# Where the block transposes of e stand in a unit: behind the first two fifths of its MLP work instead of in front of it

## The chip, the core and the metric

The kernel runs on one core of one Trainium2 chip. The metric is the device time of one execution in microseconds (us). Engines are named as in the profile: PE is TensorE (PEld its weight loads), DVE is VectorE, ACT is ScalarE, POOL is GpSimd, SP is SyncE, which in this kernel only issues DMAs. Each engine works off its own instructions in order, and waits on semaphores where an instruction needs the work of another engine.

## The reference

Thresholded attention feeds an MLP mixer. All data are float32; B = 8, H = 8 heads, S = 576, D = 64.

```python
scores = scale * np.matmul(q, k.transpose(0, 1, 3, 2))
thresh = np.max(scores, axis=-1, keepdims=True) - tau
scores = np.where(scores >= thresh, scores, -1000000000.0)
attn = softmax(scores)
attn_out = np.matmul(attn, v)                     # (B, H, S, D)
x = attn_out.transpose(0, 2, 1, 3).reshape(B, S, H * D)
xt = x.transpose(0, 2, 1)
h = np.maximum(xt @ w_tok1, 0.0) @ w_tok2
u = x + h.transpose(0, 2, 1)
out = u + np.maximum(u @ w_ch1, 0.0) @ w_ch2
```

## The kernel before, in words

**Units.** The attention is cut into 144 units, 18 for each batch: 128 queries of two heads, or, in every ninth half-batch unit (the "s" unit), the last 64 queries of four heads. The main loop at the end of the kernel takes a unit u at a time and emits, in this order: `scores(u)` (PE matmuls L301 into PSUM, the row maximum mx on DVE L306, the bias on POOL L307); `norm(u - 1)` (two small DVE operations, L330 and L331, then POOL scales e, L334); in batches 1 to 7 the transposes of unit w = u - 2; MLP work, `fill(0.4)`; `weigh(u)` (ACT L316 and L323, with three times `fill(0.2)` in between); loads of later heads; and `values` (PE L408 and L413, then ACT L418), which multiplies the transposed weights by v for a group of units that was transposed two units ago.

**The transposes.** Batch 0 transposes e on PE (`turn`). From batch 1 on `turn_blocks` does it: one DVE instruction of 128 x 1152 transposes the 32 x 32 blocks of e into T (L368). When the last unit of a group is done (a group is two units, or one s unit), 16 DMAs on SP's queue move the blocks to their places in eT (L378); call these 16 a train. 126 units go through `turn_blocks`, in 70 trains.

**The MLP work.** When a batch's attention is complete, `push` puts its MLP steps in a list, `todo`. A token step `tok2` is two PE matmuls (L446) and one DVE addition that takes the result out of PSUM (L450); `tok1` ends in an ACT operation (L440). A channel step `ch1` is four groups of matmuls (L468) that ACT takes out (L469); a `ch2` tile is four steps of matmuls (L480, L484) that DVE copies out (L489) and SP stores (L490). Where a batch's token steps meet channel steps left over from the batch before, they are interleaved. `fill(share)` takes steps until a share of the unit's quota of PE time is used, so two fifths of a unit's MLP work come in the first call, and three times a fifth inside `weigh`. During batch 1 the DVE also unpacks weights (`weight`, L201, L205, L209).

**PSUM of the MLP.** All MLP steps take their PSUM tile from one pool, `ps_mm`, of two buffers (banks 6 and 7). Which of the two a tile gets is decided when the program is built. Usually the two alternate; in some places a tile gets the buffer of the tile just before it, and its first matmul then waits until that one has been taken out.

These are the lines of the main loop that the change touches, with the two callees of interest:

```python
        if back:
            key, place, many = group_of(w)
            if in_blocks(key[0]):
                turn_blocks(w)
...
        if b_now:
            fill(0.4)
        weight(2 if b_now else 1)
        if on:
            weigh(u)
```

Of the kernel before, what the change touches and what calls it, by code (L numbers as in the profile page):

```python
# [21 lines left out]
def kernel(  # L22
# [144 lines left out]
    def load_piece(i):  # L167
        if i >= len(pieces):
            return
        dst, src = pieces[i]  # L170
        rows = dst.shape[0]
        n = 1
        for d in dst.shape[1:]:
            n *= d
        raw = raw_at[i % NRAW][0:rows, 0 : n * (2 if wide(i) else 1)].bitcast(src.dtype)
        nc.sync.dma_start(out=like(raw, dst), in_=src)
        if wide(i):
            words = raw.bitcast(U32).rearrange("p (n w) -> p n w", w=2)
            h2 = work.tile([P, WMAX], F32, tag="o", name=f"h2_{i}")[0:rows, 0:n]
            raws[i] = like(words[:, :, 0], dst), like(words[:, :, 1], dst), like(h2, dst)  # L180
        else:
            raws[i] = like(raw, dst)
# [4 lines left out]
    def on_scalar(i, part):  # L187
        if wide(i):
            lo, hi, h2 = raws[i]
            if part == 0:  # L190
                nc.scalar.activation(out=lo.bitcast(I32), in_=lo, func=AF.Copy, scale=2.0**-29)
            else:
                nc.scalar.activation(out=h2, in_=hi.bitcast(F32), func=AF.Square)

    def on_vector(i, part):
        if wide(i):
            dst = pieces[i][0]
            lo, hi, h2 = raws[i]
            bits = dst.bitcast(U32)
            if part == 0:  # L200
                nc.vector.tensor_scalar(  # L201
                    out=bits, in0=hi, scalar1=3, scalar2=0x3FFFFFFF, op0=ALU.logical_shift_left, op1=ALU.bitwise_and
                )
            elif part == 1:
                nc.vector.scalar_tensor_tensor(  # L205
                    out=bits, in0=hi, scalar=0xC0000000, in1=bits, op0=ALU.bitwise_and, op1=ALU.bitwise_or
                )
            else:
                nc.vector.scalar_tensor_tensor(out=dst, in0=h2, scalar=2.0**-30, in1=dst, op0=ALU.is_ge, op1=ALU.mult)  # L209

    def on_gpsimd(i):
        if i >= 0:
            dst = pieces[i][0]
            if wide(i):
                nc.gpsimd.tensor_tensor(out=dst.bitcast(I32), in0=dst.bitcast(I32), in1=raws.pop(i)[0].bitcast(I32), op=ALU.add)
            else:
                nc.gpsimd.tensor_copy(out=dst, in_=raws.pop(i))
# [5 lines left out]
    def weight(n):  # L223

        nonlocal steps_done
        for k in range(steps_done, min(steps_done + n, 3 * len(pieces) + 1)):
            i, part = divmod(k, 3)
            if part == 0:
                on_gpsimd(i - 1)
                if i:  # L230
                    load_piece(i - 1 + NRAW)
            else:
                on_scalar(i + 1, part - 1)
            on_vector(i, part)
            steps_done = k + 1
# [39 lines left out]
    def in_blocks(b):  # L275
        return b > 0
# [10 lines left out]
    def scores(u):  # L287
        b, p0, t = units[u]
        sc = [
            (ps_3rd if b == 0 and (2 * u + h) % 3 == 2 else ps_sc).tile([P, 2, MAIN], F32, tag="sc", name=f"sc{h}_{u}") for h in range(2)  # L290
        ]
        if t == SHARED:
            parts = [(b * NP + p0 + i, slice(MAIN, S), slice(64 * i, 64 * i + 64)) for i in range(2)]
        else:
            i, c = divmod(t - (t > SHARED), NI)
            parts = [(b * NP + p0 + i, slice(P * c, P * c + P), slice(0, P))]
        order = [(f, part, h) for f in range(2) for part in parts for h in range(2)]
        for f, (n, cols, rows), h in order if b else sorted(order, key=lambda o: o[2]):
            r = slice(D * h, D * h + D)
            qT, kT = heads[n]  # L300
            nc.tensor.matmul(sc[h][rows, f, 0:HS], lhsT=qT[r, cols], rhs=kT[r, HS * f : HS * f + HS], start=True, stop=True)  # L301
        mx = small.tile([P, 2], F32, tag="mx", name=f"mx_{u}")
        bias = small.tile([P, 2], F32, tag="bias", name=f"bias_{u}")
        for h in range(2):
            c = slice(h, h + 1)
            nc.vector.tensor_reduce(out=mx[:, c], in_=sc[h][:, :, 0:HS], axis=AX.XY, op=ALU.max)  # L306
            nc.gpsimd.tensor_scalar(out=bias[:, c], in0=mx[:, c], scalar1=toff, scalar2=-SCALE, op0=ALU.add, op1=ALU.mult)  # L307
        st[u] = sc, bias
# [28 lines left out]
    def group_of(u):  # L337

        b, p0, t = units[u]
        if t == SHARED:  # L340
            return (b, p0, "s"), 0, 1
        i, c = divmod(t - (t > SHARED), NI)
        return (b, p0 + i, c // 2), c % 2, 2
# [17 lines left out]
    def turn_blocks(u):  # L361

        key, place, n = group_of(u)
        e = st.pop(u)
        if place == 0:
            Ts[key] = work.tile([P, NK * 2 * P], F32, tag="T", name=f"T_{u}")
        T = Ts[key][:, 0 : NK * n * P]
        nc.vector.transpose(  # L368
            out=T.rearrange("p (a c n x) -> p c a n x", a=4, c=NK, n=n)[:, :, :, place, :],
            in_=e.rearrange("p (c a x) -> p c a x", c=NK, a=4),  # L370
        )
        if place == n - 1:
            del Ts[key]
            eTs[key] = work.tile([P, NK * 2 * P], F32, tag="eT", name=f"eT_{u}")
            w = NK * n * 32
            for a in range(4):
                for i in range(4):
                    nc.sync.dma_start(  # L378
                        out=eTs[key][32 * a : 32 * a + 32, w * i : w * i + w], in_=T[32 * i : 32 * i + 32, w * a : w * a + w]
                    )  # L380

    def split_middle(n):

        lv, vl = vals[n], vlast[n % VL]
        for h in range(2):
            r = slice(D * h, D * h + D)
            nc.gpsimd.tensor_copy(out=vl[r, r], in_=lv[r, NI, :])
        vals[n] = lv, vl
# [116 lines left out]
    def fill(share):  # L505
        nonlocal credit
        credit += share * quota
        while todo and credit > 0:
            cost, step = todo.popleft()
            credit -= cost  # L510
            step()
        if not todo:
            credit = 0.0
# [20 lines left out]
    for u in range(len(units) + LAG + 4):  # L534
        on = u < len(units)
        if u == UB:
            late.close()
            ps_mm = ctx.enter_context(tc.tile_pool(name="ps_mm", bufs=2, space=bass.MemoryType.PSUM))
        if on:
            b_now, p0, t = units[u]  # L540
            n = b_now * NP + p0
        w = u - LAG
        back = 0 <= w < len(units)
        if on:
            scores(u)
        if 0 < u <= len(units):
            norm(u - 1)
        if b_now:
            weight(2)
        if back:  # L550
            key, place, many = group_of(w)
            if in_blocks(key[0]):
                turn_blocks(w)
            else:
                for i in range(3):
                    turn(w, i)
            if place == many - 1:
                b, p, c = key
                if c == 0 and p % 2 == 0:
                    split_middle(b * NP + p)  # L560
                if c == "s":
                    split_middle(b * NP + p + 1)
                when = u + (2 if in_blocks(b) else 1)
                due += [(when, b, p + i, c) for i in range(2 if c == "s" else 1)]
        if b_now:
            fill(0.4)
        weight(2 if b_now else 1)
        if on:
            weigh(u)
        elif b_now:  # L570
            fill(0.6)
        weight(2 if b_now else 1)
        if on:
            m = n + 2 + t // 4
            if t < 8 and m < len(pairs):
                load_qk(m, (nc.scalar if b_now else nc.sync,) * 2, t % 4)
                if t % 4 == 3:
                    load_v(m)
            if t == 2:
                prep(n + 1)  # L580
            if t == 7 and n + 2 < len(pairs):
                prep(n + 2)
        while due and due[0][0] <= u:
            _, b, p, c = due.popleft()
            values(b, p, c)
            if p == NP - 1 and c == 1:
                push(b)
# [31 lines left out]
```

## Time and profile before

| what | value |
|---|---|
| median of 3 runs | 1394.02 us (1393.48 to 1395.14) |
| the profiled execution, its own time | 1392.27 us |
| span of its profile | 1390.5 us |
| granted TensorE clock, mean | 0.991 |
| DVE busy | 586.8 us, 42% of the span |
| ACT busy | 590.0 us, 42% |
| POOL busy | 357.8 us, 26% |
| transposes T<-e, L368 | x126, 1369 ns each |
| additions xT<-xT,t, L450 | x64, 441 ns each |
| copies o<-c, L489 | x36, 679 ns each |
| DMA issues eT<-T, L378 | x1120 on SP, about 2.0 us from issue to landing |

The span runs from the first to the last instruction; the 1.8 us between it and the time of the same execution lie around it. A row of the timeline reads: start in us, length in us, engine, line, operation, what is written and read, number of instructions merged in the row, and in brackets the idle time of the engine before it and what ended that. A row of the waits reads: who waited for whom, then us in total, times, and the longest in us.

### The profile page before, as it was taken

How to read it: one execution, taken by the hardware profiler on the slowest of the kernel's cores; microseconds unless marked ns; L12 is line 12 of the kernel's file. 1: busy time of each engine (PE TensorE's matmuls, PEld its weight loads, DVE VectorE, ACT ScalarE, POOL GpSimd, SP SyncE). 2: the span in 40 equal slices, each digit the busy share in tenths (PEclk: the TensorE clock that was granted, in tenths of full speed). 3: DMA queues.
4: the chain of work that ended last, by engine and by line, in shares of the span. 5: the costliest groups of instructions: out<-in, count | busy, mean ns of one | idle time of the engine just before them, and what ended most of it. 6: DMA issues, size and time to landing. Idle time of an engine off the chain costs nothing.

```text
span 1390.5 us, 19515 instructions
## 1 busy us (share of the span) xinstructions
PE 1325.5 (95%) x6866; PEld 831.8 (60%) x6866; DVE 586.8 (42%) x1009; ACT 590.0 (42%) x1328; POOL 357.8 (26%) x683
## 2 busy tenths in 40 slices
PE   6776899999999999999999999999999999999998
PEld 3443475646565566665766567465657566575675
DVE  6788784444444444434244344433343453101000
ACT  5776564444454444443434435353434444120110
POOL 4566563232222222212122222221221222000000
PEclk9998899999999999999999999999999999999999
DMA  6444654444444434433433444443433433300000
GB/s 132 97 115 125 185 140 122 109 120 93 107 118 107 105 86 97 109 84 79 110 85 92 104 96 102 98 105 79 99 91 89 103 76 85 84 8 16 8 8 23
DMA packets 257376, 128.34 MB, mean 92 GB/s; under 512 B 208064, under 2 KB 221376, under 8 KB 257280
## 3 DMA queue, kind: packets, MB, share of 16 engines
q1 hardware_dynamic: 131632, 111.46, 30.5%
q10 hardware_dynamic: 125648, 15.64, 7.1%
q8 instruction: 55, 0.90, 0.3%
q14 instruction: 41, 0.34, 0.1%
HBM read 43.25 MB, written 9.44 MB: 38 GB/s over the span
## 4 chain that ended last, share of the span: by engine, by line
PE 86%; DVE 6%; DMA 2%; ACT 2%; SPq 2%; POOL 1%; issue 1%; DVEq 0%; ACTq 0%
PE c L484 27%; PE c L468 26%; PE sc L301 11%; PE pv L413 7%; PE t L439 5%; PE t L446 3%; PE pv L408 2%; DVE mx L306 2%; PE tx L430 1%; SPq L378 1%; PE c L480 1%; PE pv_s L413 1%; DVE T L368 1%; DMA scratch<-in_moe_w_ch_dram 1%; ACT e L316 1%
## 5 line engine op out<-in xcount | busy, mean ns | idle before, releaser
L306 DVE TENSOR_REDUCE mx<-sc 128x1 f32<-128x576 f32 x288 | 204.7, 751 | 523.1 <-PE sc L301 521.1
L468 PE MATMUL c<-xT,wc 128*128 128x256 f32 (+1 forms) x1920 | 398.6, 361 | 0.5 <-ACT g L469 0.4
L484 PE MATMUL c<-wc,g 128*128 128x512 f32 x864 | 389.1, 596 | 0.0
L468 PEld LDWEIGHTS c<-xT,wc 128*128 128x128 f32 x1920 | 334.3, 190 | 69.7 <-issue 27.6
L307 POOL TENSOR_SCALAR bias<-mx,toff 128x1 f32<-128x1 f32 x288 | 79.6, 277 | 814.9 <-DVE mx L306 757.9
L316 ACT ACTIVATE e<-sc,bias 128x576 f32<-128x576 f32 x288 | 199.2, 739 | 155.5 <-POOL bias L307 155.1
L484 PEld LDWEIGHTS c<-wc,g 128*128 128x128 f32 x864 | 157.9, 190 | 175.3 <-issue 173.2
L469 ACT ACTIVATE g<-c 128x256 f32<-128x256 f32 (+1 forms) x240 | 86.7, 361 | 335.5 <-PE c L468 330.6
L334 POOL TENSOR_SCALAR e<-e,rr 128x576 f32<-128x576 f32 x288 | 218.8, 772 | 16.0 <-DVE rr L331 3.8
L323 ACT ACTIVATE e<-e,ntau 128x576 f32<-128x576 f32 x288 | 220.6, 771 | 0.0
L301 PE MATMUL sc<-kT,qT 64*128 64x288 f32 (+1 forms) x1280 | 190.1, 435 | 14.2 <-DVE kT L283 7.2
L368 DVE STREAM_TRANSPOSE T<-e 128x1152 f32<-128x1152 f32 x126 | 172.5, 1369 | 16.3 <-DMA eT<-T 9.6
L301 PEld LDWEIGHTS sc<-kT,qT 64*128 64x128 f32 (+1 forms) x1280 | 103.7, 179 | 90.0 <-issue 47.6
L413 PE MATMUL pv<-eT,lv 128*64 128x256 f32 x1024 | 123.5, 384 | 0.0
L413 PEld LDWEIGHTS pv<-eT,lv 128*64 128x64 f32 x1024 | 75.1, 139 | 37.5 <-issue 0.8
L489 DVE COPY o<-c 128x512 f32<-128x512 f32 x36 | 24.5, 679 | 160.8 <-PE c L484 160.8
L446 PE MATMUL t<-w,a 128*128 128x288 f32 x256 | 79.0, 438 | 13.6 <-DVE xT L450 10.4
L418 ACT COPY xT<-pv 128x256 f32<-128x256 f32 x64 | 23.8, 372 | 160.0 <-PE pv L413 147.2
L439 PE MATMUL t<-x_sb,w 128*128 128x512 f32 x160 | 73.2, 605 | 0.7 <-ACT g L469 0.7
L446 PEld LDWEIGHTS t<-w,a 128*128 128x128 f32 x256 | 46.8, 198 | 41.4 <-DVE xT L450 18.4
L450 DVE TENSOR_TENSOR xT<-xT,t 128x288 f32<-128x288 f32 x64 | 28.0, 441 | 81.9 <-PE t L446 81.9
L323 ACT ACTIVATION_READ_ACCUMULATOR e<-e,ntau 128x1 f32 x288 | 56.5, 196 | 0.0
(48 smaller groups left out, 603.2 us busy)
## 6 DMA issues: line engine op xcount, KB each, us to landing
eT<-T SPq DMA_DIRECT2D x896, 72.0 KB, 2.1
scratch<-in_moe_w_ch_dram SPq DMA_DIRECT2D x24, 512.0 KB, 4.0
lv<-in_v_dram SPq DMA_DIRECT2D x32, 288.0 KB, 3.3
out_dram<-o SPq DMA_DIRECT2D x36, 256.0 KB, 2.2
eT<-T SPq DMA_DIRECT2D x224, 36.0 KB, 1.9
lk<-in_k_dram ACTq DMA_DIRECT2D x108, 72.0 KB, 2.8
lq<-in_q_dram ACTq DMA_DIRECT2D x104, 72.0 KB, 2.1
lq<-in_q_dram SPq DMA_DIRECT2D x24, 72.0 KB, 3.4
```

The source lines that it names most:

```text
L301: nc.tensor.matmul(sc[h][rows, f, 0:HS], lhsT=qT[r, cols], rhs=kT[r, HS * f : HS * f + HS], start=True, stop=True)
L306: nc.vector.tensor_reduce(out=mx[:, c], in_=sc[h][:, :, 0:HS], axis=AX.XY, op=ALU.max)
L316: nc.scalar.activation(out=eh, in_=sc[h][:, :, 0:HS], func=AF.Prelu, bias=bias[:, h : h + 1], scale=SCALE, alpha=STEEP)
L323: nc.scalar.activation(out=eh, in_=eh, func=AF.Exp, bias=ntau, accum_out=rs[:, h : h + 1])
L334: nc.gpsimd.tensor_scalar(out=eh, in0=eh, scalar1=rr[:, h : h + 1], scalar2=1.0, op0=ALU.mult, op1=ALU.mult)
L368: nc.vector.transpose(out=T.rearrange("p (a c n x) -> p c a n x", a=4, c=NK, n=n)[:, :, :, place, :], in_=e.rearrange("p (c a x) -> p c a ...
L413: nc.tensor.matmul(to[r], lhsT=lv[:, j, :], rhs=eT[:, j], start=False, stop=(c == NI - 1), skip_group_check=True)
L439: nc.tensor.matmul(ps, lhsT=w1[:, t, P * m : P * m + P], rhs=x_sb[:, t, :], start=(t == 0), stop=(t == NT - 1))
L446: nc.tensor.matmul(ps, lhsT=s["a"][:, m, P * c : P * c + P], rhs=w2[:, m, HS * f : HS * f + HS], start=(m == 0), stop=(m == NTK - 1))
L468: nc.tensor.matmul(ps, lhsT=wc1[:, j, c, :], rhs=uT[:, c, GR * i : GR * i + n], start=(c == 0), stop=(c == NCC - 1))
L469: nc.scalar.activation(out=s["g"][:, j, 0:n], in_=ps, func=AF.Relu)
L484: nc.tensor.matmul(flat, lhsT=s["g"][:, j, P * t : P * t + P], rhs=wc2[:, j, :], start=False, stop=(j == NJ - 1), skip_group_check=True)
```

## The change

`turn_blocks(w)` is emitted behind `fill(0.4)` instead of in front of it. Batch 0's `turn` and the list of due `values` stay where they were; no instruction is added or taken away.

```diff
         if back:
             key, place, many = group_of(w)
-            if in_blocks(key[0]):
-                turn_blocks(w)
-            else:
+            if not in_blocks(key[0]):
                 for i in range(3):
                     turn(w, i)
             if place == many - 1:
...
         if b_now:
             fill(0.4)
+        if back and in_blocks(key[0]):
+            turn_blocks(w)
         weight(2 if b_now else 1)
         if on:
             weigh(u)
```

## The prediction, made before the changed kernel had been run

> **What bounds the kernel now.** I read the page's busy times first, then its slices.
>
> ```profile
> PE 1325.5 (95%) x6866; PEld 831.8 (60%) x6866; DVE 586.8 (42%) x1009; ACT 590.0 (42%) x1328; POOL 357.8 (26%) x683
> PE   6776899999999999999999999999999999999998
> PEclk9998899999999999999999999999999999999999
> ```
>
> PE is full from the sixth slice on (a slice is 34.8 us), and DVE, on which the moved instruction runs, is busy 42%. So a DVE instruction costs or gains time only where PE waits for what stands behind it. The waits of PE alone, from 140 to 1200 us, which covers the stretch with block transposes, show all there is to win:
>
> ```profile
> PE t L446 <- DVE xT L450: 10.4, 8, 2.6
> PE t L446 <- ACT g L469: 3.1, 6, 0.8
> PE sc L301 <- ACT e L316: 1.9, 1, 1.9
> PE c L480 <- ACT g L469: 0.7, 2, 0.4
> PE t L439 <- ACT g L469: 0.7, 2, 0.4
> PE c L468 <- ACT g L469: 0.4, 1, 0.4
> ```
>
> The first row is 10.4 us in eight waits for the token step's addition. The four ACT g rows, 4.9 us, look foreign to a change on DVE; I come back to them. The timeline at one wait of the first kind:
>
> ```profile
> 315.83 2.21 PE L446 MATMUL t<-w,a 128*128 128x288 f32 x8
> 317.46 0.17 DVE L331 RECIPROCAL rr<-rr 128x2 f32<-128x2 f32 x1
> 317.55 1.36 DVE L368 STREAM_TRANSPOSE T<-e 128x1152 f32<-128x1152 f32 x1
> 318.83 0.78 DVE L450 TENSOR_TENSOR xT<-xT,t 128x288 f32<-128x288 f32 x2
> 319.30 3.18 PE L446 MATMUL t<-w,a 128*128 128x288 f32 x12 [1.26 <-DVE xT L450]
> ```
>
> Two token steps fill both PSUM buffers by 318.04; the additions that would free them stand behind the transpose, which nothing needs soon. PE restarts 0.47 us after the addition's start. A wait also costs the overlap of two matmuls: L446 lasts 0.41 us but starts every 0.24 us, so a closed gap of 1.26 returns up to 1.42.
>
> **What moves.** In the order of the built programs PE, ACT and POOL have the same instructions in the same order. On DVE only 31 of the 126 transposes pass anything, because in the other units the first two fifths hold no DVE work: 19 pass one or two token additions, ten pass a copy o<-c, two pass one of each. Nothing passes a later unit's mx. On SP 8 of the 70 trains pass an output transfer. Dropped work: none; added work: none; so the sum consists of waits alone.
>
> **Where the addition is freed.** In each case the addition takes the transpose's start, and PE restarts 0.47 to 0.48 after that or when its previous matmuls end, whichever is later.
> - At 317.63: restart 318.03, returned 1.27; then the transpose lies 318.3 to 319.7 and holds the next addition, and the third step after loses about 0.1. Net 1.15.
> - At 326.69: addition at 326.60 instead of 328.23; 1.6.
> - At 489.3: addition at 488.25 (it doesn't share the transpose's 0.24 wait); all 0.79 of the gap and the overlap, 0.95.
> - At 620.8 and 944.7: 0.50 gap each, wholly, 0.67; two smaller delays of 0.16 in each of these batches (a matmul starting late without a listed gap) go too: 2.0 together.
> - At 477.0: the addition frees its step (1.04), but here the built program gives the next channel step the same buffer, so it waits for an addition of 0.45 and two hand-overs, estimated at 0.70. Net 0.35.
>
> **The ACT rows.** Here the position of the transpose decides the buffer:
>
> ```profile
> 803.42 1.05 PE L468 MATMUL c<-xT,wc 128*128 128x128 f32 x8
> 804.07 1.36 DVE L368 STREAM_TRANSPOSE T<-e 128x1152 f32<-128x1152 f32 x1
> 804.52 0.28 ACT L469 ACTIVATE g<-c 128x128 f32<-128x128 f32 x1 [2.95 <-PE c L468]
> 804.85 1.24 PE L446 MATMUL t<-w,a 128*128 128x288 f32 x4 [0.37 <-ACT g L469]
> 805.35 0.42 DVE L450 TENSOR_TENSOR xT<-xT,t 128x288 f32<-128x288 f32 x1
> ```
>
> The step at 804.85 has the buffer of the channel step just finished, and must wait until ACT has taken that out. In the changed program nine tiles that had their predecessor's buffer get the other one (one before, four in each of batches 4 and 6), and one tile (the one at 477) newly gets its predecessor's. The step at 804.85 then waits for the addition before it, moved to 804.07: restart 804.55, 0.30 returned. The same at 814.7 (0.29, and 0.24 at the next step) and 822.7 (0.30). At 780.4 the tile waits for a copy o<-c that also leaves the transpose's shadow: 0.45. That is 1.58 per batch, twice 3.2. The tile at 498 gets 0.5. The wait of 0.83 at 799 stays: there ACT is late by a bias, in both programs.
>
> **Batch 1's start, and the clock.** Gaps of 2.58 at 150.24 and 2.33 at 163.83 lie in the stretch where DVE unpacks weights. The first only moves: its transpose passes one addition of two, and the other stays at 154.5 behind L209 and L201, so the second next step starts at 155.0 as before: 0. At the second both additions pass; the first channel step then starts at about 168.5 instead of 169.8. DVE is busy 9.79 of 10 us at 175 to 185, and mx at 172.87 had waited only 1.04 for PE, so I carry 1.0 on. The windows there:
>
> ```profile
> 152.82:160.00 7.18, 7.18 (x26) 4.06 (x28) 4.34 (x7) 5.13 (x10) 2.30 (x2) 0.56 0.75 199
> 166.17:169.40 3.23, 3.23 (x7) 2.37 (x8) 2.19 (x4) 0.00 (x0) 3.06 (x4) 0.51 0.82 253
> ```
>
> The third number from the right is the granted clock: 0.56 and 0.51 after these gaps, some (1 - 0.56) x 7.18 = 3.2 and 1.6 us of PE time. The Trainium skill ("TensorE: Matmul & The Clock Gate", the section "Why this matters for your kernels") asks for no idle gaps over about 3 us; by it gaps of 2.6 and 2.3 cost no clock and shrinking them returns none. By the rows they do cost it, and up to 3 us more could return in the first stretch (the second's loss is inside the 1.0). Because the first stretch's idle time is only split, 1.3 and 2.4 us, I take 0 and keep 3 for the range. Below zero: if the halved window falls later, up to 1.0 is lost.
>
> **What comes later.** The moved transpose is 1.37 us; it delays additions of the last three fifths only where they follow within 1.4 us, which I found once (the 0.1 above), since steps of 1.1 to 2.7 us alternate. The next mx comes at least 4 us later. A copy o<-c is waited for on DVE, and the transpose with its train behind it: at 391.15 the transpose goes behind the copy of 392.43 (due at 392.3), so it starts 1.75 later, its train with it. That train's 16 issues take 10.56 us from 392.57, the last lands about 2 later, at 405.0, and its reader on PE starts at 408.34: 3.3 us to spare, 1.5 left. That is the least of all 19 moved trains; the others have 3.9 to 12.8, and an output transfer in front takes 0.53 of SP. So 0. The e buffer is needed by ACT a unit later: 0.
>
> **Sum.** 1.0 + 1.15 + 1.6 + 0.35 + 0.95 + 2.0 + 0.5 + 3.2 = 10.75 us. The profiled execution took 1392.27 (span 1390.5 and 1.8 around it), so 1381.5 of its kind; it lay 1.75 under the median of the runs. Against that median: 1394.02 - 10.8 = 1383.2.
>
> **The rivals.**
> - The stall only changes its place: additions in the last three fifths stand behind the transpose instead, and PE meets the other one. For it: the 477 case, the 0.1 above and the first gap of batch 1. Against: the spacing. Half of it happening gives 1388.5; all of it 1394.
> - Slower: the trains come late. They share SP's queue with output transfers, which wait for copies (SP waited 197.3 us for o in 16 waits), and 8 trains now stand behind one. From 3.3 us of added delay on, PE waits at the reader. If those eight trains slipped by 6 us and cost 2 to 3 each, 16 to 24 less 10.8 gives 1399 to 1407, middle 1403. Against: a copy's own matmuls are done within 3 us of the unit's scores.
> - No effect, because PE's listed gaps are filled elsewhere anyhow (a later wait absorbs them): from 200 to 1200 the units' PE work follows without other listed waits, so only batch 1's start could be absorbed. All absorbed: 1394.
> - More: the clock comes back in batch 1 and the overlap everywhere: 14 us, 1380.
>
> **Chances.** 0.2% is 2.8 us, about what a measurement of this kernel can tell from no change. Forecast case (1380.5 to 1387) 0.66; more than that 0.09; half returned (1387 to 1391.2) 0.11; moved or no effect 0.08; slower 0.06. Faster 0.86, same 0.08, slower 0.06. The range from 1378.0 to 1390.5 leaves out the last two cases and the edges.
>
> **What would show it.** In the profile after, PE's waits from 170 to 1200 us should fall from 5.5 (of the 10.4) to about 2 for xT, and from 4.9 to 1.7 for g, while those before 170 keep some 5 in shorter pieces; restarts near 318.0, 326.9 and 489.4 (less what is gained before) without a gap. PE's waits for eT should stay absent. Wrong: gaps of 0.5 to 1.4 at L446 or L468 with DVE as releaser in the later fifths, a listed PE wait on DMA eT<-T, or a second halved clock window beyond 170 us.

## The result

The changed kernel takes 1383.19 us (median of six runs, 1382.55 to 1385.04), the kernel before 1393.03 in six runs on the same chips: 9.8 us less, a ratio of 0.9931 with an interval from 0.9918 to 0.9943. The prediction on record was 1383.2.

The page of the changed kernel's profile, busy times, then PE's slices and clock. Its span is 1383.3 us, its own time 1385.04, the longest of its six runs:

```profile
PE 1324.6 (96%) x6866; PEld 831.8 (60%) x6866; DVE 586.7 (42%) x1009; ACT 590.3 (43%) x1328; POOL 359.4 (26%) x683
PE   5776899999999999999999999999999999999998
PEclk9997999999999999999999999999999999999999
```

Every engine has the same instructions as before, so the 7.2 us between the two spans lie in waits and in the stretches in which PE's clock was halved. PE's waits in the changed kernel from 140 to 1200 us:

```profile
PE t L446 <- DVE xT L450: 3.3, 3, 1.3
PE sc L301 <- ACT e L316: 1.9, 1, 1.9
PE c L468 <- DVE xT L450: 1.8, 2, 1.2
PE t L446 <- ACT g L469: 1.7, 2, 0.8
PE c L468 <- ACT g L469: 1.2, 1, 1.2
PE tx L430 <- ACT x_sb L431: 0.2, 1, 0.2
```

Token steps wait 3.3 us for additions instead of 10.4, and 1.7 for ACT instead of 3.1; the rows for c L480 and t L439 behind ACT are gone. Two rows are new: channel steps behind an addition (1.22 us at 171.56, 0.55 at 479.57), and 1.25 us behind ACT at 188.48.

Two spans of single executions can't be subtracted without care here. The row maximum mx of unit 28 marks the end of the stretch in which weights are unpacked. Its row before:

```profile
196.14 1.42 DVE L306 TENSOR_REDUCE mx<-sc 128x1 f32<-128x576 f32 x2 [0.38 <-PE sc L301]
```

and in the changed kernel:

```profile
199.53 1.42 DVE L306 TENSOR_REDUCE mx<-sc 128x1 f32<-128x576 f32 x2 [1.90 <-PE sc L301]
```

The changed kernel is 3.4 us later there, and yet 7.2 earlier at the end: from this mark to the end it needs 1383.3 - 199.5 = 1183.7 us instead of 1194.3. The 3.4 us are older than the change: at unit 19, before any moved transpose, the changed kernel was already 3.8 behind; it had 13.7 us of halved clock up to there, the kernel before 3.4. With the mx rows of units 19 and 28 as marks, all profiles fall into three stretches:

| kernel | to unit 19 | 19 to 28 | 28 to the end | runs, median | ratio to before (interval) |
|---|---|---|---|---|---|
| before | 111.5 | 84.7 | 1194.3 | 1393.03 | |
| changed | 115.3 | 84.3 | 1183.7 | 1383.19 | 0.9931 (0.9918 to 0.9943) |
| changed_again | 112.3 | 86.0 | 1183.7 | 1384.27 | 0.9936 (0.9923 to 0.9948) |
| order_only | 112.2 | 84.9 | 1186.2 | 1385.12 | 0.9944 (0.9931 to 0.9958) |
| buffers_only | 112.2 | 86.3 | 1200.7 | 1400.45 | 1.005 (1.0037 to 1.0062) |
| from_batch_2 | 111.9 | 84.6 | 1183.7 | 1382.21 | 0.9928 (0.9915 to 0.994) |
| behind_all_fills | 112.4 | 94.4 | 1186.9 | 1392.57 | 0.999 (0.9977 to 1.0003) |
| one_buffer_more | 111.1 | 83.7 | 1182.9 | 1381.04 | 0.9909 (0.9895 to 0.9923) |
| loads_on_pool | 112.0 | 84.4 | 1184.1 | 1382.99 | 0.9924 (0.9909 to 0.9939) |
| all_fills_and_pool_loads | 111.5 | 83.3 | 1187.7 | 1385.3 | 0.9946 (0.9932 to 0.9959) |
| buffer_and_pool_loads | 115.4 | 84.2 | 1183.3 | 1382.5 | 0.9925 (0.9911 to 0.9938) |

The first stretch holds no block transpose of the changed part and varies by 4.3 us between executions. The last repeats to 0.1 us in the three profiles whose programs agree there (changed, changed_again and from_batch_2, each 1183.7). So the last stretch tells apart what the medians blur.

### The profile page after: what moved, and what is told of

Its sections match the earlier page's. It is cut to its first block, busy times and chain, and to the rows that moved or that the text cites. A ratio compares the mean times of both kernels' runs of the same rounds, so it can differ in the third digit from the quotient of the medians.

```text
span 1383.3 us, 19517 instructions
## 1 busy us (share of the span) xinstructions
PE 1324.6 (96%) x6866; PEld 831.8 (60%) x6866; DVE 586.7 (42%) x1009; ACT 590.3 (43%) x1328; POOL 359.4 (26%) x683
## 3 DMA queue, kind: packets, MB, share of 16 engines
q1 hardware_dynamic: 131632, 111.46, 30.7%
## 4 chain that ended last, share of the span: by engine, by line
PE 89%; DVE 5%; DMA 1%; POOL 1%; ACT 1%; issue 1%; SPq 0%; ACTq 0%; DVEq 0%
PE c L484 27%; PE c L468 27%; PE sc L301 11%; PE pv L413 8%; PE t L439 5%; PE t L446 4%; PE pv L408 3%; DVE mx L306 2%; PE tx L430 1%; PE c L480 1%; PE pv_s L413 1%; DMA scratch<-in_moe_w_ch_dram 1%; POOL wc L215 1%; DVE eT L359 1%; ACT e L316 1%
## 5 line engine op out<-in xcount | busy, mean ns | idle before, releaser
L468 PE MATMUL c<-xT,wc 128*128 128x256 f32 (+1 forms) x1920 | 398.6, 361 | 3.0 <-DVE xT L450 1.8
L468 PEld LDWEIGHTS c<-xT,wc 128*128 128x128 f32 x1920 | 334.4, 190 | 72.1 <-issue 28.8
L301 PE MATMUL sc<-kT,qT 64*128 64x288 f32 (+1 forms) x1280 | 190.2, 434 | 17.1 <-ACT e L316 10.0
L446 PE MATMUL t<-w,a 128*128 128x288 f32 x256 | 77.5, 431 | 5.3 <-DVE xT L450 3.3
L439 PE MATMUL t<-x_sb,w 128*128 128x512 f32 x160 | 72.5, 600 | 0.0
L446 PEld LDWEIGHTS t<-w,a 128*128 128x128 f32 x256 | 46.7, 196 | 30.6 <-issue 11.9
```

Of the source, the lines that this page charges most:

```text
L439: nc.tensor.matmul(ps, lhsT=w1[:, t, P * m : P * m + P], rhs=x_sb[:, t, :], start=(t == 0), stop=(t == NT - 1))
L446: nc.tensor.matmul(ps, lhsT=s["a"][:, m, P * c : P * c + P], rhs=w2[:, m, HS * f : HS * f + HS], start=(m == 0), stop=(m == NTK - 1))
L468: nc.tensor.matmul(ps, lhsT=wc1[:, j, c, :], rhs=uT[:, c, GR * i : GR * i + n], start=(c == 0), stop=(c == NCC - 1))
```

## The profile after, at two of the predicted places

Where the prediction showed two additions behind a transpose (then at 317.5 to 319.3), the timeline of the changed kernel has:

```profile
319.23 2.96 PE L446 MATMUL t<-w,a 128*128 128x288 f32 x10
320.86 0.17 DVE L331 RECIPROCAL rr<-rr 128x2 f32<-128x2 f32 x1
320.94 0.98 DVE L450 TENSOR_TENSOR xT<-xT,t 128x288 f32<-128x288 f32 x2
321.85 1.37 DVE L368 STREAM_TRANSPOSE T<-e 128x1152 f32<-128x1152 f32 x1
```

The additions come at the end of the reciprocal, the transpose after them, and PE's row runs through. Where a step had waited for ACT because of its buffer (then at 804.85):

```profile
800.41 1.05 PE L468 MATMUL c<-xT,wc 128*128 128x128 f32 x8
801.05 0.43 DVE L450 TENSOR_TENSOR xT<-xT,t 128x288 f32<-128x288 f32 x1
801.40 1.37 DVE L368 STREAM_TRANSPOSE T<-e 128x1152 f32<-128x1152 f32 x1
801.50 0.28 ACT L469 ACTIVATE g<-c 128x128 f32<-128x128 f32 x1 [2.95 <-PE c L468]
801.53 1.24 PE L446 MATMUL t<-w,a 128*128 128x288 f32 x4
```

The token step starts 0.03 us after ACT has begun to take the channel step out, so it no longer waits for that: it starts 0.48 after the start of the addition, in the other buffer.

## The experiments

**Order and buffers apart.** The theory has two parts: additions and copies that leave the transpose's shadow (order), and nine tiles that stop taking their predecessor's buffer (buffers). To separate them, the pool is replaced by two pools of one buffer each, and the tiles that keep their predecessor's buffer are listed by number.

```diff
-            ps_mm = ctx.enter_context(tc.tile_pool(name="ps_mm", bufs=2, space=bass.MemoryType.PSUM))
+            ps_mm = TwoPools([ctx.enter_context(tc.tile_pool(name=f"ps_mm{i}", bufs=1, space=bass.MemoryType.PSUM)) for i in range(2)])
...
+        def tile(self, *args, **kw):
+            if self.n not in SAME:
+                self.at = 1 - self.at
+            self.n += 1
+            return self.pools[self.at].tile(*args, **kw)
```

order_only has the changed order with the list of before. On record was:

> The transposes stand behind the first two fifths, as in the changed kernel, but each MLP tile gets the PSUM buffer that it had before the change. Theory (two parts: additions freed from behind the transposes, and nine tiles that no longer take their predecessor's buffer): the second part is missing, so the PE waits of 0.37 us for ACT g come back at four tiles in each of two batches and at one more, and the new wait of 0.55 us for an addition is gone. From the steps between the two traces that is 1.03 + 1.60 + 1.06 + 2.6 + 1.04 + 2 x 0.24 = 7.8 of 10.6 us: about 1385.5, ratio 0.9944. Rival (the freed additions do it all, the buffers are incidental): as the changed kernel, ratio 0.993 or a little better.

Measured: 1385.12 us, 0.9944; from unit 28 to the end 8.1 of the 10.6 us. PE's waits of order_only, the rows behind ACT g, from 140 to 1230 us:

```profile
PE t L446 <- ACT g L469: 3.1, 6, 0.8
PE c L468 <- ACT g L469: 0.8, 2, 0.4
PE c L480 <- ACT g L469: 0.7, 2, 0.4
PE t L439 <- ACT g L469: 0.7, 2, 0.4
```

The rows for t L446, c L480 and t L439 are those of before. The buffers are worth the difference, 1186.2 - 1183.7 = 2.5 us; this is the net of nine tiles that gain and one, at 479, that loses.

buffers_only has the order of before with the changed list. On record was:

> The order of before, but each MLP tile gets the PSUM buffer that it has in the changed kernel. Theory (the buffers pay only where the addition or copy that frees them is no longer behind the transpose): PE now waits for additions that stand behind a transpose, about 1 us longer than it waited for ACT at three tiles in each of two batches, 0.4 less at the fourth, and 0.6 and 0.7 at two single tiles: some 6.5 us slower than before, 1399.5, ratio 1.0047. Rival (the better buffers are a gain of their own, 2.8 us): ratio 0.998.

Measured: 1400.45, 1.005; from unit 28 on 6.4 us slower than before. The waits of buffers_only in the same window:

```profile
PE t L446 <- DVE xT L450: 17.0, 13, 2.3
PE c L480 <- DVE xT L450: 2.7, 2, 1.3
```

Before, the first of these rows had 10.4 us in eight waits, and there was none for c L480. The waits for ACT have been traded for longer ones for additions that stand behind transposes. So the same buffers cost 6.4 us in the one order and return 2.5 in the other: they are no gain of their own.

**Batch 1.** from_batch_2 leaves all transposes of batch 1 in front, among them the two that had passed additions. Its edit of the changed kernel:

```diff
-            if not in_blocks(key[0]):
+            if key[0] == 1:
+                turn_blocks(w)
+            elif not in_blocks(key[0]):
...
-        if back and in_blocks(key[0]):
+        if back and key[0] > 1:
```

> As the changed kernel, but in batch 1, where two transposes had passed additions, they stay in front of the MLP work; batches 2 to 7 as changed. Theory (what these two moves return is lost again 20 us later, where ACT waits for a weight load): same as the changed kernel within 0.5 us, ratio 0.993. Rival (1.0 us is kept, as predicted, or up to 3 more by the clock): 1 to 4 us slower than the changed kernel, ratio 0.9938 to 0.996.

> The changed kernel itself, on the same chip as the other three: 1383.2, ratio 0.993.

Measured, on one chip: 1382.21 and 1384.27. The stretch from unit 19 to 28 takes 84.6 us in from_batch_2, 84.3 and 86.0 in two executions of the changed kernel, and 84.7 before: nothing that these two moves return can be seen. The theory's time came out, its reason did not: PE waits 1.26 us for ACT at unit 27 here too, with nothing moved in batch 1. What became of the second move, the changed kernel's timeline of PE and DVE shows:

```profile
168.13 2.21 PE L446 MATMUL t<-w,a 128*128 128x288 f32 x8 [1.07 <-DVE xT L450]
168.36 1.36 DVE L368 STREAM_TRANSPOSE T<-e 128x1152 f32<-128x1152 f32 x1
169.65 1.11 DVE L209 SCALAR_TENSOR_TENSOR wc<-h,wc 128x512 f32<-128x512 f32 x1
170.69 0.45 DVE L201 TENSOR_SCALAR wc<-scratch 128x512 uint32<-128x512 uint32 x1
171.06 0.81 DVE L450 TENSOR_TENSOR xT<-xT,t 128x288 f32<-128x288 f32 x2
171.56 1.99 PE L468 MATMUL c<-xT,wc 128*128 128x256 f32 x8 [1.22 <-DVE xT L450]
```

The token step waits 1.07 us instead of 2.33, but the next two additions now stand behind the transpose and two operations that unpack weights, and the channel step behind them waits 1.22: 2.29 in all. With the transpose in front, in from_batch_2, PE's rows at the same place are:

```profile
166.31 2.21 PE L446 MATMUL t<-w,a 128*128 128x288 f32 x8 [2.33 <-DVE xT L450]
168.47 1.99 PE L468 MATMUL c<-xT,wc 128*128 128x256 f32 x8
```

and in the kernel before:

```profile
166.17 3.77 PE L446 MATMUL t<-w,a 128*128 128x288 f32 x8 [2.33 <-DVE xT L450]
169.78 1.89 PE L468 MATMUL c<-xT,wc 128*128 128x256 f32 x8
```

Counted from the mx row of unit 24, the channel step starts after 6.61 us in the changed kernel, after 6.60 in from_batch_2 and after 8.05 before. The two orders come out equal. Before has the order and the wait of from_batch_2 at this place and differs by the clock, which was halved, so that eight matmuls took 3.77 us instead of 2.21.

**Behind all of the MLP work.** behind_all_fills moves the transposes three fifths further:

```diff
-        if back and in_blocks(key[0]):
-            turn_blocks(w)
...
         elif b_now:
             fill(0.6)
+        if back and in_blocks(key[0]):
+            turn_blocks(w)
```

> The transposes go behind the whole of a unit's MLP work (behind weigh), not only behind the first two fifths. 49 transposes pass something instead of 31, 21 trains start about 3 to 5 us later than in the changed kernel. Theory: nearly all that can be returned was returned by the first two fifths, and the trains' spare time (in the trace of the changed kernel 1.6 to 13 us between the last landing and the reader) is now used up at a few readers; also two tiles get their predecessor's buffer back (0.3 each). So 0.5 to 4 us slower than the changed kernel, 1384 to 1387, ratio 0.9935 to 0.996, with PE waits behind DMA eT<-T. Rival (the trains have room, and the later fifths' additions return as much as the first's did): 2 us or more faster than the changed kernel, ratio 0.9915.

Measured: 1392.57 (twelve runs), 0.999: the gain is gone, where I had expected less than half of that loss. The profile is that of its slowest run (1395.52), so its sizes may be on the high side. PE's waits for the late trains alone are a small part, as its rows from 140 to 1230 us show:

```profile
PE c L468 <- ACT g L469: 6.7, 1, 6.7
PE t L446 <- DVE xT L450: 3.8, 2, 2.7
...
PE pv L408 <- DMA eT<-T: 0.7, 2, 0.4
PE pv_s L408 <- DMA eT<-T: 0.6, 1, 0.6
```

The readers of eT wait 1.3 us, one place behind ACT 6.7. Its timeline, of SP, ACT and PE:

```profile
178.74 10.01 SPq L378 DMA_DIRECT2D eT<-T  x16
...
188.91 0.93 SPq L176 DMA_DIRECT2D scratch<-in_moe_w_ch_dram  x2
...
192.88 0.68 ACT L191 ACTIVATE scratch<-scratch 128x512 int32<-128x512 uint32 x1 [5.23 <-DMA scratch<-in_moe_w_ch_dram]
...
193.45 0.37 ACT L469 ACTIVATE g<-c 128x256 f32<-128x256 f32 x1
193.88 2.21 PEld L468 LDWEIGHTS c<-xT,wc 128*128 128x128 f32 x6 [7.08 <-ACT g L469]
193.88 2.50 PE L468 MATMUL c<-xT,wc 128*128 128x256 f32 x5 [6.68 <-ACT g L469]
```

A train holds SP for 10.0 us; two weight loads queue behind it and land when ACT has waited 5.2 us for one; the operation that would free PE's buffer stands behind that on ACT. The changed kernel has the same at the same unit, with less to lose:

```profile
170.68 11.20 SPq L378 DMA_DIRECT2D eT<-T  x16
...
181.99 1.50 SPq L176 DMA_DIRECT2D scratch<-in_moe_w_ch_dram  x3
...
186.07 0.69 ACT L191 ACTIVATE scratch<-scratch 128x512 int32<-128x512 uint32 x1 [5.12 <-DMA scratch<-in_moe_w_ch_dram]
...
188.05 0.38 ACT L469 ACTIVATE g<-c 128x256 f32<-128x256 f32 x1
...
188.48 1.99 PE L468 MATMUL c<-xT,wc 128*128 128x256 f32 x8 [1.25 <-ACT g L469]
```

**The loads on another queue.** From batch 1 on, POOL issues the weights' loads:

```diff
-        nc.sync.dma_start(out=like(raw, dst), in_=src)
+        (nc.gpsimd if b_now else nc.sync).dma_start(out=like(raw, dst), in_=src)
```

> The changed kernel, but from batch 1 on the weights' loads are issued from POOL's queue instead of SP's, where they stand behind trains. Theory (batch 1's returned time is lost at unit 27, where ACT waits for a weight load that stood behind a train on SP): that wait of ACT (5.1 us) and PE's of 1.25 behind it go, 1 to 3 us less, 1381.5, ratio 0.992. Rival (DVE's own full queue at 175 to 200 us is the limit): unchanged, 0.993; or slower, 0.995, if issuing on POOL delays the biases.

> The transposes behind the whole of the MLP work, with the weights' loads from batch 1 on issued from POOL's queue. Theory (7 of the 8 us that the later place costs come from weight loads that stand behind a later train on SP, for which ACT, and then PE, waits 6.7 us at unit 27): that wait goes, and what is left over the changed kernel is 1.3 us at three readers of eT and 2.4 at PSUM tiles, so about 1385, ratio 0.9945. Rival (the loss at unit 27 is DVE's or the train's own, not the loads'): the wait stays, ratio 0.999.

In all_fills_and_pool_loads the time falls from 1392.57 to 1385.3, as expected, and each of its five runs is faster than each of the twelve of behind_all_fills. So some 7 us of the later place's loss hang on the queue of the loads; the order on DVE and PE is the same in both. Where they were lost is shown less well. The stretch from 19 to 28 falls from 94.4 to 83.3 us, but only 5.1 of these 11.1 lie behind unit 25 (32.1 to 27.0), and the rest lies where the profiles scatter. The wait of 6.68 did not go, as expected, but fell to 3.14 (lines from L176 on have a number one higher in this kernel):

```profile
182.51 0.37 ACT L419 COPY xT<-pv 128x256 f32<-128x256 f32 x1 [7.31 <-DMA eT<-T]
...
183.78 1.99 PE L469 MATMUL c<-xT,wc 128*128 128x256 f32 x8 [3.14 <-ACT g L470]
```

ACT had stood still for 7.31 us, by the profile until a DMA of a train landed, so what is left here goes back to a train and not to a load. From unit 28 on the kernel needs 1187.7 us, near the 1186.9 without the loads' move and 4.0 more than the changed kernel.

On the changed kernel itself the same edit takes PE's wait for ACT at unit 27 away: from unit 25 to 28 (mx row to mx row) loads_on_pool and buffer_and_pool_loads take 23.3 us, and the changed kernel takes 24.8 and 24.1 in its two profiles. Yet the time is 1382.99, not told from the changed kernel. Part of that wait was given back elsewhere: unit 19 takes 9.06 us in all three kernels with the loads on POOL and 8.56 to 8.58 in the eight others, and the last stretch is 0.4 us longer. Why is not shown.

**One buffer more, and both mendings together.** In one_buffer_more the one tile that newly took its predecessor's buffer, at 479 us, alternates again (its number leaves the list).

> The changed kernel with one tile's PSUM buffer swapped: the channel step that newly got its predecessor's buffer (the PE wait of 0.55 us at 479) alternates again. Theory: that wait goes, 0.7 us less, which the times hardly show (ratio 0.9925 against 0.993) but the wait's row does. Rival (the wait only moves to the next tile): ratio 0.993 and another row of the same size.

The 0.55 us wait is gone, and 28 to the end is 0.8 us shorter, 1182.9. Its median of 1381.04 is lower than that explains; the part up to unit 28, which differs between executions, was the shortest of all in its profile, 194.8 us, with 13.7 us of halved clock where the changed kernel had 30.7. Both mendings together:

> The changed kernel with both small mendings: one more tile alternates its buffer, and the weights' loads from batch 1 on go through POOL's queue. Theory: both are kept, 0.8 and about 1 us: about 1 to 2 us less than the changed kernel, 1381 to 1382, ratio 0.991 to 0.992, faster than both kernels. Rival (batch 1's differences are noise of the clock windows): ratio 0.9925.

Measured: 1382.5, 0.9925, 1183.3 from unit 28 on. The intervals of both versions overlap those of the changed kernel, so neither is shown to beat it; what stands is the buffer's 0.8 us in the last stretch, from 1183.7 to 1182.9 and, with the loads on POOL, from 1184.1 to 1183.3.

## Why the prediction was right, and where it was not

From the marks of the units, the steps of its sum against the two profiles:

| step of the prediction | predicted | from the traces |
|---|---|---|
| batch 1, with the clock at 0 | 1.0 | 0 |
| 317.6 | 1.15 | 1.03 |
| 326.7 | 1.6 | 1.60 |
| 477 | 0.35 | 0.33 |
| 489 | 0.95 | 1.06 |
| 498 | 0.5 | 0.64 |
| batches 3 and 5 (620, 944 and the small ones) | 2.0 | 2.6 |
| batches 4 and 6 (780 to 823, 1104 to 1146) | 3.2 | 3.4 |
| sum | 10.75 | 10.6 (unit 28 to the end) |

- The forecast's mechanism holds from batch 2 on, in both parts: order_only returns 8.1 us by the order alone, and the buffers add 2.5 to it.
- The step that failed is the first: 1.0 carried on from batch 1. The prediction let both additions pass at the wait of 2.33 us and had the first channel step start at 168.5 instead of 169.8. It left out that this step waits for the next two additions, which then stand behind the transpose: 2.33 became 1.07 and 1.22, and 0.04 us came back. The 1.3 us that it saw there in the trace of before were the halved clock's, as from_batch_2 shows, which reaches the same point without the move. What else limits the 85 us from unit 19 to 28 stays open.
- So the rival "the stall only changes its place" was right for batch 1 (the gap of 2.58, too, became two of 0.91 and 1.32, which the prediction had expected), and one of the prediction's signs of being wrong is there, the gap of 1.22 at L468 behind DVE. The other two are not: no PE wait for eT, and no halved clock beyond 170 us. Later it happened once with a size: 0.55 us at 479, which was in the sum.
- The small delays of batches 3 and 5 were 0.26 each and not 0.16, and the waits at 620 and 944 0.77 and not 0.67; with smaller misses at 489, 498 and in batches 4 and 6 this made up for batch 1. That the sum fits to 0.2 us is partly luck.
- The median to start from was also off: before has 1393.03 in six runs and not 1394.02 in three, so the measured gain is 9.8 and not 10.8, with 7.9 to 11.4 in its interval. The start was about 1 us too high and the gain about 1 us larger than the medians give; that 1383.2 was hit so closely is luck.
- "Trains come late" was the right danger at the wrong victim. In the changed kernel the least spare time before a reader of eT is 1.6 us, as worked out (1.5), and no reader waits. Three fifths further down, three readers wait 1.3 us in all; some 7 us went when the weights' loads no longer stood behind trains on SP. The prediction had asked only for the train's own readers.
- The 3 us that were kept for the clock did not show: between units 19 and 25 the changed kernel had 17.1 us of halved clock in one profile and 23.9 in the other, and before had 20.5.

## What to carry to other kernels

An instruction that nobody needs soon belongs behind the short ones that free a buffer for the busy engine. The gain can be read off beforehand, one listed wait at a time, if for each the next thing that the busy engine waits for is looked up as well: from batch 2 on the sum came to 10.6 us where 9.75 were expected, and in batch 1, where the next additions followed right behind, to nothing. When instructions are moved, the framework may hand out the buffers of a pool differently: compare the buffers of both programs, since the same hand-out returned 2.5 us in one order and cost 6.4 in the other. And of a moved step with DMAs, ask for everything that stands behind those on the issuing queue, not only for the reader of their data.

## What the runs showed of the hardware

PE's clock was halved after stalls shorter than 3 us, but not after every one, and at other places in each execution. The windows of the changed kernel at three stretches of 3.4 us; the third number from the right is the granted clock:

```profile
151.50:155.00 3.50, 3.50 (x8) 2.33 (x8) 3.17 (x7) 1.45 (x4) 1.90 (x4) 0.51 1.04 308
155.00:158.40 3.40, 1.55 (x6) 0.68 (x4) 3.40 (x6) 1.26 (x3) 2.24 (x3) 1.00 0.97 283
158.40:161.80 3.40, 3.02 (x8) 1.71 (x10) 1.39 (x4) 3.40 (x8) 1.11 (x1) 0.50 0.91 258
```

PE was busy 1.55 of 3.40 us in the second stretch, with waits of 0.91 and 1.32 us (the second ends 0.4 later), and the clock was halved in the third. The prediction put the halved clock that followed the gap of 2.33 us down to that gap. The same gap in from_batch_2 was followed by this:

```profile
166.31:169.60 3.29, 3.29 (x13) 2.46 (x14) 3.16 (x6) 0.00 (x0) 3.07 (x4) 1.00 0.86 229
```

So the length of a gap alone does not decide it; what does is not shown here. In all profiles the halved stretches last 3.4 us or a multiple, apart from those cut off at the end of the profile. One of them cost 1.3 us where all else was the same: unit 24, from its mx row to the next, took 11.14 us before, with 3.4 us of halved clock, and 9.80 in from_batch_2, with none. From unit 19 to 25 the time follows them (the two kernels with the transposes behind all of the MLP work left out): 58.0 us with 10.2 us of halved clock, 59.5 to 61.1 with 17.1, 60.9 and 61.4 with 20.5, 61.9 and 63.1 with 23.9. These sums alone don't tell cause from effect, since waits may come first; the pair at unit 24 does for its place. So the clock is one of the reasons why the part before unit 28 differs by several us between executions, and a sum of waits there is worth less than one from the rest.
